# Two-bank cumulative sums, fp32 sums at the start, work moved to GpSimd and a new issue order, in a gated recurrence followed by a GEGLU mixture layer

## The chip, the cores and the metric

The kernel runs on one core of a Trainium2 chip. The core's engines are called PE (TensorE, the matrix products), ACT (ScalarE, the functions), DVE (VectorE), POOL (GpSimd) and SP (SyncE, here only a queue of DMA issues). Each runs its own list of instructions in order and waits on semaphores for the others. The metric is the time of one launch in microseconds (us), the median over several runs. Before the change that is 261.7 us (three runs, 261.25 to 261.72).

## The reference

Inputs q, k, v, a_re, a_im are 4 batches x 8 heads x 768 steps x 48 channels in float32. A complex decay a = a_re + i a_im, its magnitude held at 0.999 or less, drives a state for each batch and head, and the state is read with q:

```python
mag = np.sqrt(a_re * a_re + a_im * a_im)
scale = np.minimum(mag, 0.999) / (mag + 1e-06)
a_re_n, a_im_n = (a_re * scale, a_im * scale)
for t in range(S):
    new_re = ar * S_re - ai * S_im
    new_im = ar * S_im + ai * S_re
    kv = k[:, :, t] outer v[:, :, t]
    S_re, S_im = (new_re + kv, new_im)
    y[:, :, t] = q[:, :, t] @ S_re
```

(ar and ai are column t of a_re_n and a_im_n, the two products are written here without their index strings.) The 3072 x 384 result x goes through a gated feed-forward layer with 1536 hidden channels:

```python
g = x @ w_gate
gelu = 0.5 * g * (1.0 + erf(g * inv_sqrt2))
val = x @ w_val
ffn_out = gelu * val @ w_out
res_gate = 1.0 / (1.0 + np.exp(-(x @ w_res)))
return (x + res_gate * ffn_out)
```

## The kernel before

**Tiling.** The 768 steps are cut into 6 chunks of 128. A tile is one chunk of one batch: 128 steps in the partitions, 8 heads x 48 = 384 channels along the free dimension. There are 24 tiles, worked in units: the first chunk of batches 0 and 1 singly, that of batches 2 and 3 as a pair, then pairs for each later chunk, and the very last pair as two single units again. That makes 14 units, 10 pairs (128 x 768 operands) and 4 singles (128 x 384). For each unit three functions record steps.

**prepare(p)** loads ar, ai, q, k, vf (L373, SP, 192 KB for each tile) and computes log magnitude and angle of the decay and their running sums. ACT takes ln of ar (L394) into la and exp of its negative (L395); t = exp * ai (tai, L397); the square (L399 on ACT, L401 on DVE); ln(1 + s) (L402); la = 0.5 s + la (L403, DVE). la is capped and split into a rounded part lh (L406) and a rest ll (L408), both in the fast float32 matrix type. PE multiplies each with an upper triangle of ones (L359, two products of 128 x 384 for each tile, summed in PSUM), which gives the running sum along the steps. ACT makes E = exp of it (L423) and Ei = exp of its negative (L424), one instruction for each tile. E's last row goes out to the small tile mr by a DMA on POOL's queue (mrd, L428). The angle t = arctan(t) (L433) gets the angle carried over from the previous chunk added to its first row by a DMA on POOL's queue (carry, L439 or L445); it is split into th and tl (L334 copy and L452) and summed in the same way; "round" (L462, ACT) writes the nearest number of full turns as an integer and "fr" (L464, DVE) takes the turns off, one instruction each for each tile. abs (L471 or L473) and two sines (L477) give sine and cosine in CS. DVE multiplies q by E and k by Ei (qe, L482) and both by CS (feat, L487) to the feature tiles fQ and fK, whose heads have 96 channels. These are transposed to QT and KT, for part of the tiles on PE (L504) with a copy on ACT or DVE (L333, L334), for others by a DMA transpose on SP.

**attend(p)** makes the scores of QT and KT for each head (L535), masks them (am, L538), multiplies with v (L547) and with the state (L549), builds the products of features and v (L559) and carries the state on: U (L565), Gb in bfloat16 (L567, DVE) and Gf in float32 (L572). The copies of the result x (L333, L334) end it.

**forward(p)** transposes x (L591 on PE, or by DMA on SP, L583), forms gate and value products (gv, L605) of two of the twelve column tiles of 128 at a time into one PSUM bank each, gelu on ACT (L610) and its product with the value on DVE (h, L611); the residual gate (L620, tanh L622); the output product in three groups of four (L631); ot (L635, DVE), the sum with x (otx, L638, POOL or DVE) and the store (L640). In a pair a bank holds 2 x 256 columns; in a single unit 2 x 128, half a bank.

**The order of the work.** Steps aren't issued as they are recorded. ORDER lists all of them by number and fixes the order on every engine; PLACE sets by step number the engine of those steps that can run on more than one. When a step is issued, its buffers are chosen from what is free (25 wide ones of 128 x 768 float32, tag "wd"; eight PSUM banks, tag "pb"; smaller ones). Where the function set of ACT changes, a table load is issued (L652). The weights wg, wv, wr and wo are loaded by DMAs on POOL's queue (L340), whose issues stand between POOL's other work as ORDER has them. And steps of DVE and POOL whose kind is in PORT are made to take turns by semaphores:

```python
if t.kind in PORT and t.eng in ("DVE", "POOL"):
    other = turn.get("POOL" if t.eng == "DVE" else "DVE")
    if other is not None:
        after(ins, other)
    turn[t.eng] = ins
```

Of the kernel before, what the change touches and what calls it, by code (L numbers as in the profile page):

```python
# [9 lines left out]
FP = mybir.dt.float32  # L10
# [11 lines left out]
SL, ST = 1,1  # L22
WD = 25
# [7 lines left out]
    24: "DVE", 33: "DVE", 40: "DVE", 50: "DVE", 51: "ACT", 53: "ACT", 64: "ACT", 104: "POOL", 114: "ACT", 116: "POOL",  # L31
    132: "ACT", 145: "ACT", 190: "DVE", 191: "DVE", 203: "DVE", 213: "DVE", 223: "DVE", 225: "ACT", 236: "DVE", 252: "ACT",
    305: "DVE", 306: "DVE", 318: "DVE", 322: "ACT", 323: "POOL", 330: "DVE", 340: "DVE", 345: "DVE", 347: "ACT", 353: "DVE",
    422: "DVE", 435: "DVE", 438: "POOL", 446: "DVE", 460: "DVE", 463: "ACT", 551: "DVE", 554: "POOL", 555: "POOL", 562: "DVE",
    572: "DVE", 576: "DVE", 585: "DVE", 595: "DVE", 667: "DVE", 670: "ACT", 671: "POOL", 686: "ACT", 688: "DVE", 692: "DVE",
    771: "DVE", 786: "POOL", 787: "POOL", 821: "DVE", 866: "DVE", 872: "DVE", 899: "DVE", 902: "POOL", 903: "POOL", 910: "DVE",
    933: "DVE", 984: "DVE", 1014: "ACT", 1015: "POOL", 1050: "DVE", 1088: "DVE", 1121: "ACT", 1124: "POOL", 1125: "POOL",
    1151: "DVE", 1160: "DVE", 1198: "DVE", 1232: "POOL", 1233: "POOL", 1240: "DVE", 1251: "ACT", 1257: "DVE", 1304: "DVE",
    1325: "POOL", 1329: "DVE", 1344: "DVE", 1376: "DVE", 1396: "ACT", 1397: "POOL", 1410: "ACT", 1448: "DVE",
}  # L40
ORDER = [
    97, 98, 16, 102, 293, 17, 103, 410, 104, 21, 105, 22, 106, 294, 23, 24, 411, 179, 115, 295, 34, 35, 116, 296, 117, 107, 25,
    178, 118, 303, 26, 36, 420, 27, 37, 108, 119, 28, 100, 181, 180, 413, 304, 109, 120, 421, 110, 305, 121, 38, 29, 188, 30,
    111, 39, 306, 412, 307, 32, 99, 182, 189, 308, 112, 309, 190, 31, 125, 191, 319, 310, 101, 526, 41, 321, 122, 40, 19, 18,
    123, 320, 42, 113, 183, 299, 204, 422, 124, 205, 127, 130, 33, 527, 423, 436, 206, 43, 207, 528, 20, 529, 184, 44, 126, 314,
    192, 46, 128, 316, 193, 210, 45, 322, 208, 424, 194, 47, 195, 49, 211, 323, 131, 129, 199, 52, 196, 209, 48, 536, 315, 311,
    212, 324, 135, 425, 50, 537, 1, 185, 298, 137, 437, 54, 200, 132, 114, 138, 538, 312, 136, 198, 325, 313, 326, 426, 55, 327,
    300, 759, 297, 186, 758, 53, 7, 141, 56, 133, 197, 539, 139, 328, 643, 642, 213, 134, 201, 214, 51, 329, 60, 438, 140, 57,
    216, 439, 58, 144, 202, 2, 187, 330, 215, 334, 12, 552, 217, 8, 332, 553, 6, 0, 219, 331, 218, 226, 336, 142, 220, 768, 333,
    143, 222, 227, 145, 224, 62, 440, 761, 645, 644, 301, 302, 225, 335, 441, 223, 769, 554, 221, 242, 343, 443, 59, 555, 61,  # L50
    339, 243, 63, 240, 652, 64, 344, 444, 341, 233, 231, 442, 241, 228, 234, 317, 244, 445, 653, 146, 760, 337, 5, 342, 232,
    559, 540, 340, 874, 4, 654, 3, 245, 150, 235, 154, 560, 338, 556, 875, 561, 236, 85, 170, 360, 87, 152, 350, 156, 166, 203,
    345, 148, 361, 81, 354, 65, 171, 9, 10, 168, 446, 11, 83, 229, 162, 427, 73, 13, 164, 158, 77, 67, 75, 351, 417, 416, 160,
    557, 89, 355, 541, 79, 90, 69, 358, 74, 431, 558, 230, 71, 151, 318, 359, 770, 251, 364, 348, 365, 66, 155, 153, 349, 433,
    428, 432, 68, 362, 429, 14, 76, 363, 771, 430, 163, 655, 346, 82, 86, 70, 147, 84, 78, 347, 157, 656, 149, 249, 72, 165,
    167, 252, 159, 237, 172, 250, 884, 367, 15, 238, 357, 257, 91, 885, 88, 169, 269, 352, 80, 562, 542, 784, 447, 657, 92, 415,
    253, 239, 161, 448, 261, 543, 414, 273, 173, 366, 93, 353, 563, 564, 668, 877, 369, 174, 658, 450, 876, 434, 669, 254, 94,
    175, 368, 452, 263, 255, 449, 258, 265, 277, 259, 455, 986, 419, 418, 278, 451, 459, 267, 533, 988, 279, 256, 886, 785, 457,
    456, 275, 453, 458, 274, 280, 454, 1206, 370, 670, 435, 659, 372, 464, 374, 386, 460, 271, 671, 246, 465, 530, 382, 887,
    276, 260, 248, 1097, 388, 376, 390, 466, 461, 467, 384, 474, 476, 480, 544, 95, 1207, 392, 247, 531, 356, 475, 786, 547,  # L60
    270, 371, 468, 545, 532, 477, 548, 549, 787, 272, 469, 675, 1096, 772, 373, 262, 266, 281, 481, 987, 773, 546, 1216, 672,
    660, 534, 646, 989, 484, 535, 176, 676, 264, 268, 888, 550, 677, 478, 470, 788, 471, 479, 791, 566, 889, 663, 462, 662, 661,
    792, 96, 673, 282, 793, 287, 1106, 674, 375, 996, 568, 565, 288, 283, 463, 789, 665, 997, 485, 387, 567, 1107, 664, 647,
    473, 284, 177, 289, 391, 571, 575, 573, 377, 389, 285, 790, 900, 396, 394, 649, 648, 577, 290, 551, 678, 1098, 393, 486,
    998, 679, 572, 569, 286, 574, 680, 510, 570, 506, 487, 378, 764, 291, 576, 901, 681, 1208, 592, 650, 488, 774, 490, 511,
    397, 775, 1099, 502, 380, 492, 383, 590, 482, 683, 504, 498, 508, 591, 385, 593, 881, 651, 1306, 1209, 902, 582, 491, 999,
    395, 500, 903, 689, 379, 489, 586, 685, 381, 493, 483, 690, 1000, 594, 398, 583, 1108, 686, 776, 779, 907, 765, 595, 778,
    580, 587, 399, 581, 781, 780, 908, 1217, 596, 794, 601, 400, 904, 578, 682, 584, 472, 777, 880, 292, 1378, 684, 404, 905,
    597, 499, 1109, 579, 585, 909, 600, 1218, 687, 1311, 503, 688, 628, 691, 405, 762, 401, 763, 599, 666, 906, 1122, 696, 890,
    507, 692, 706, 795, 402, 698, 406, 505, 697, 501, 403, 693, 512, 699, 1379, 878, 1012, 589, 520, 610, 509, 1219, 796, 911,  # L70
    708, 494, 407, 1013, 618, 707, 408, 602, 709, 879, 614, 782, 598, 798, 513, 612, 629, 620, 992, 995, 1123, 604, 496, 1307,
    616, 495, 710, 700, 603, 766, 797, 891, 895, 767, 892, 619, 896, 799, 497, 1001, 521, 701, 893, 1383, 910, 716, 615, 800,
    1384, 711, 617, 1385, 1312, 894, 897, 605, 522, 783, 913, 1014, 514, 801, 611, 802, 810, 805, 898, 1313, 515, 806, 882, 717,
    1124, 523, 702, 607, 703, 621, 712, 516, 1015, 912, 1230, 613, 803, 606, 726, 804, 517, 1215, 899, 1002, 914, 993, 883, 994,
    990, 622, 1003, 608, 807, 728, 667, 588, 734, 811, 915, 808, 738, 730, 722, 991, 917, 736, 723, 916, 732, 624, 609, 814,
    623, 824, 713, 918, 740, 724, 815, 812, 822, 1314, 1016, 1004, 1213, 625, 813, 725, 825, 1220, 1006, 1019, 823, 1007, 727,
    694, 731, 524, 518, 1125, 809, 1033, 695, 1020, 1315, 729, 816, 1017, 525, 920, 919, 1021, 636, 817, 1018, 704, 1009, 1008,
    1005, 1316, 735, 1025, 519, 1102, 828, 718, 626, 637, 705, 720, 733, 737, 714, 926, 638, 1231, 1386, 832, 826, 1022, 639,
    719, 818, 630, 1026, 827, 627, 1308, 1210, 833, 1100, 927, 640, 715, 829, 1322, 721, 1129, 631, 1024, 936, 1126, 924, 937,
    641, 921, 632, 1394, 925, 1127, 739, 1232, 1130, 819, 633, 1381, 1023, 928, 1128, 929, 1028, 744, 752, 746, 934, 742, 747,  # L80
    753, 842, 1027, 1221, 1131, 1387, 1110, 741, 409, 831, 935, 1031, 1032, 1323, 1395, 844, 1309, 1030, 846, 754, 1132, 938,
    1222, 944, 939, 1317, 1111, 1112, 848, 743, 1223, 858, 834, 847, 1103, 836, 1113, 945, 745, 859, 1045, 838, 748, 930, 755,
    634, 835, 840, 1029, 1046, 849, 1324, 1114, 1047, 922, 830, 1212, 1048, 1133, 843, 1117, 1233, 1211, 1101, 635, 923, 931,
    1134, 837, 839, 1224, 950, 845, 1325, 1105, 1310, 749, 1038, 850, 1318, 1119, 1116, 1118, 841, 1319, 1115, 1136, 1104, 1320,
    1036, 1039, 946, 851, 966, 756, 1321, 1225, 1037, 1226, 1049, 757, 1135, 1380, 854, 972, 1050, 821, 852, 1214, 948, 853,
# [21 lines left out]
class Store:  # L107


    def __init__(self, tag, bufs):  # L110
        self.tag, self.bufs, self.users, self.tile, self.index = tag, bufs, [], None, None
# [75 lines left out]
def kernel(  # L187
# [13 lines left out]
    nc = tc.nc  # L201
# [78 lines left out]
    class Wide(Val):  # L280
# [7 lines left out]
        def tile(self):  # L288
            if self.store.tile is None:
# [3 lines left out]
                elif self.name in ("E", "Ei", "fr", "fw"):  # L293
                    x = x[:, :].rearrange("p (c m) -> p c m", c=2)
# [388 lines left out]
```

## Time and profile before

| what | value |
| --- | --- |
| median of three runs | 261.7 us (261.25 to 261.72) |
| the profiled execution | 262.78 us, of which the span of the core is 261.0 |
| mean granted PE clock | 0.978 |
| PE busy | 226.4 us, 87% |
| DVE busy | 225.4 us, 86% |
| ACT busy | 214.1 us, 82% |
| POOL busy | 94.5 us, 36% |
| largest DMA queue (SP's) | 35.53 MB, 79.4% of 16 engines |
| gate and value products (L605) | 1008, together 115.1 us busy |
| output products (L631) | 288, 56.5 us busy |
| table loads (L652) | 36, 1.283 us each |

The lines are read so. Busy time counts the instructions themselves, not the waits. PE's products overlap, so the mean length of one is longer than its share of the time (an output product: 326 ns mean, four in 0.65 us on the chain). In the slices of the span each digit is the busy share in tenths, and PEclk the granted clock in tenths. The chain of waits lists from the end backwards what each piece of work waited for.

### The profile page before, as it was taken

What the parts mean: (1) busy time and instruction counts of PE and PEld (TensorE: products, weight loads), DVE (VectorE), ACT (ScalarE), POOL (GpSimd) and SP (SyncE); (2) the same over time, 40 slices, a digit from 0 to 9 for tenths busy, and PEclk for the clock granted to TensorE, in tenths of its full rate; (3) what the DMA queues carried; (4) which work ended last, traced back from release to release, by engine and by line L of the source; (5) the groups of instructions that cost most, each with busy time, mean ns of one, the idle gap of its engine ahead of it and who ended that gap; (6) DMA issues with size and microseconds to landing.
All of it is one profiled execution on the core that took longest, in us unless ns stands there. A gap on an engine that the chain in (4) does not pass through costs nothing.

```text
span 261.0 us, 6358 instructions
## 1 busy us (share of the span) xinstructions
PE 226.4 (87%) x2426; PEld 181.8 (70%) x2426; DVE 225.4 (86%) x404; ACT 214.1 (82%) x355; POOL 94.5 (36%) x114
## 2 busy tenths in 40 slices
PE   0230992889999999999999999999999999999993
PEld 0120772778978977877878877778778777887881
DVE  2589889999899999999999999999999794965363
ACT  4999999899899999999998999999988684241240
POOL 3013086196605743576625634351420001110110
PEclk9999996599999999999999999999999999999998
DMA  8999999989999997995989896999757919402111
GB/s 141 187 187 186 187 194 192 213 163 213 202 184 172 167 186 163 221 146 124 211 149 190 148 179 149 182 168 236 133 114 160 117 23 136 133 3 63 60 63 60
DMA packets 162174, 39.83 MB, mean 153 GB/s; under 512 B 155617, under 2 KB 162145, under 8 KB 162145
## 3 DMA queue, kind: packets, MB, share of 16 engines
q1 hardware_dynamic: 157696, 35.53, 79.4%
q0 software_dynamic: 4448, 3.90, 9.3%
q8 instruction: 19, 0.31, 0.5%
q14 instruction: 11, 0.08, 0.1%
HBM read 31.26 MB, written 4.72 MB: 138 GB/s over the span
## 4 chain that ended last, share of the span: by engine, by line
PE 71%; DMA 11%; ACT 9%; DVE 3%; POOL 2%; SPq 1%; issue 1%; POOLq 0%; DVEq 0%
PE pb L605 32%; PE pb L631 17%; PE pb L359 6%; PE pb L620 4%; PE pb L504 4%; PE pb L535 3%; DMA wo<-in_moe_w_out_dram 3%; DMA wv<-in_moe_w_val_dram 2%; DMA ai<-in_a_im_dram 2%; ACT L652 2%; DMA t<-fr 2%; DMA ar<-in_a_re_dram 2%; POOL t L397 1%; PE pb L549 1%; PE pb L547 1%; ACT CS L477 1%
## 5 line engine op out<-in xcount | busy, mean ns | idle before, releaser
L610 ACT ACTIVATE h<-pb 128x512 bf16<-128x512 f32 (+1 forms) x84 | 41.2, 547 | 23.2 <-PE pb L631 13.0
L605 PE MATMUL pb<-xT,wv 128*128 128x256 bf16 (+1 forms) x504 | 58.1, 257 | 0.4 <-DMA wv<-in_moe_w_val_dram 0.4
L605 PE MATMUL pb<-xT,wg 128*128 128x256 bf16 (+1 forms) x504 | 57.0, 257 | 0.0
L631 PE MATMUL pb<-wo,h 128*128 128x384 bf16 x288 | 56.5, 326 | 0.0
L611 DVE SCALAR_TENSOR_TENSOR h<-h,pb 128x512 bf16<-128x512 bf16 (+1 forms) x84 | 48.5, 602 | 4.2 <-PE pb L605 2.8
L605 PEld LDWEIGHTS <-wg 128*128 128x128 bf16 x504 | 42.9, 98 | 7.1 <-issue 0.8
L652 ACT ACT_TABLE_LOAD x36 | 46.2, 1283 | 1.3 <-PEq L667 0.7
L605 PEld LDWEIGHTS <-wv 128*128 128x128 bf16 x504 | 41.9, 98 | 7.5 <-issue 1.3
L638 POOL TENSOR_TENSOR ot<-ot,x 128x384 f32<-128x384 f32 x16 | 14.6, 913 | 65.0 <-DVE Gb L567 23.4
L631 PEld LDWEIGHTS <-h 128*128 128x128 bf16 x288 | 26.3, 97 | 13.0 <-issue 0.4
L538 DVE TENSOR_TENSOR am<-pb,mask 128x512 bf16<-128x512 f32 x48 | 31.9, 680 | 2.9 <-PE pb L535 2.8
L397 POOL TENSOR_TENSOR t<-t,ai 128x768 f32<-128x768 f32 (+1 forms) x10 | 16.0, 1601 | 18.1 <-DVE fK L487 9.0
L504 PE MATMUL pb<-ident,fK 128*128 128x128 bf16 x112 | 10.0, 246 | 13.5 <-DVE fK L487 13.5
L359 PE MATMUL pb<-th,ut_one 128*128 128x384 f32 x24 | 11.3, 471 | 11.4 <-POOL th L334 11.1
L452 POOL TENSOR_TENSOR tl<-t,th 128x768 fp32r<-128x768 f32 (+1 forms) x10 | 16.5, 1656 | 10.4 <-DVE ll L408 7.8
L635 DVE SCALAR_TENSOR_TENSOR ot<-sg,pb 128x384 f32<-128x384 f32 x24 | 13.1, 547 | 6.8 <-PE pb L631 5.0
L504 PEld LDWEIGHTS <-fK 128*128 128x128 bf16 x112 | 8.4, 112 | 15.0 <-DVE fK L487 14.3
L535 PE MATMUL pb<-QT,KT 96*128 96x128 bf16 x192 | 17.7, 225 | 0.5 <-DMA QT<-fQ 0.4
L535 PEld LDWEIGHTS <-KT 96*128 96x128 bf16 x192 | 13.8, 101 | 3.9 <-issue 2.2
L622 ACT ACTIVATE sg<-pb 128x384 f32<-128x384 f32 x24 | 11.6, 502 | 5.3 <-PE pb L620 2.8
L620 PE MATMUL pb<-wr,xT 128*128 128x384 bf16 x72 | 15.5, 326 | 0.0
L423 ACT ACTIVATE E<-pb 128x384 f32<-128x384 f32 x24 | 11.5, 500 | 3.2 <-PE pb L359 3.0
(91 smaller groups left out, 472.2 us busy)
## 6 DMA issues: line engine op xcount, KB each, us to landing
ar<-in_a_re_dram SPq DMA_DIRECT2D x24, 192.0 KB, 4.6
ai<-in_a_im_dram SPq DMA_DIRECT2D x24, 192.0 KB, 4.6
k<-in_k_dram SPq DMA_DIRECT2D x24, 192.0 KB, 4.4
q<-in_q_dram SPq DMA_DIRECT2D x24, 192.0 KB, 4.5
vf<-in_v_dram SPq DMA_DIRECT2D x24, 192.0 KB, 4.3
out_dram<-ot SPq DMA_DIRECT2D x24, 192.0 KB, 2.8
wg<-in_moe_w_gate_dram POOLq DMA_DIRECT2D x6, 192.0 KB, 5.6
wv<-in_moe_w_val_dram POOLq DMA_DIRECT2D x6, 192.0 KB, 5.9
```

What stands on the lines that cost most here:

```text
L359: nc.tensor.matmul(out=bank.tile, lhsT=ut_one, rhs=x[:, i * DM:(i + 1) * DM], start=(j == 0), stop=(j == 1))
L397: add(e1, "tai", lambda: on[e1].tensor_tensor(out=F("t"), in0=F("t"), in1=flat(T("ai"), n), op=OP.mult), [s["ai"]], [s["t"]], n)
L452: add(e10, "tl", lambda: on[e10].tensor_tensor(out=F("tl"), in0=F("t"), in1=F("th").bitcast(FP), op=OP.subtract), [s["t"], s["th"]], [s["t ...
L504: nc.tensor.transpose(out=tp.tile[:, h, :], in_=s[g].tile[:, i * H + h], identity=ident)
L535: nc.tensor.matmul(out=ap.tile[:, h, :], lhsT=kT.tile[0:DD, u * H // 2 + h, :], rhs=qT.tile[0:DD, u * H // 2 + h, :], start=True, stop=True)
L538: add("DVE", "am", lambda u=u, am=am, ap=ap: nc.vector.tensor_tensor(out=am.tile[:, u * H // 2:(u + 1) * H // 2, :], in0=ap.tile, in1=mask ...
L605: nc.tensor.matmul(out=o_.tile[:, u, :], lhsT=w_[:, k_, (2 * m + u) * 128:(2 * m + u + 1) * 128], rhs=s["xT"].tile[:, k_, 0:n].rearrange(" ...
L610: add("ACT", "gelu", lambda gp=gp, hv=hv: nc.scalar.activation(out=hv(), in_=gp.tile, func=AF.Gelu), [gp], [hh], n, "G")
L611: add("DVE", "h", lambda vp=vp, hv=hv: nc.vector.scalar_tensor_tensor(out=hv(), in0=hv(), scalar=0.5, in1=vp.tile, op0=OP.mult, op1=OP.mul ...
L620: nc.tensor.matmul(out=rp.tile, lhsT=s["xT"].tile[:, k_, i, :], rhs=wr[:, k_, :], start=(k_ == 0), stop=(k_ == KF - 1))
L631: nc.tensor.matmul(out=op_.tile, lhsT=s["h2"].tile[:, k_, i * 128:(i + 1) * 128], rhs=wo[:, k_, :], start=(k_ == 0), stop=(k_ == NF - 1))
L652: plan.run(ORDER, lambda table: nc.scalar.preload_act_table_set(ACT_SETS[table]), after)
```

## The change

1. PSUM is one tile of eight banks, and a buffer can be one bank or an aligned pair of banks. Only the running sums of pair units take two banks (TWO = {"cum"}); E, Ei, round and fr of a pair are then one instruction each, reading both banks.
2. Units 0 to 3 (PF_L, PF_T = 4) don't split la and t. la is capped in place and multiplied in one full float32 product with a float32 triangle, t likewise.
3. The loads of ar go straight into la's buffer and ln works in place, so that no wide buffer is taken for ar.
4. In single units a gate or value step fills a whole bank (four column tiles of 128), so gelu and h work on 128 x 512 instead of 128 x 256.
5. Eighteen steps of eight products of the identity with itself are added to PE (WARM = 18), each into a PSUM bank that nothing reads.
6. The multiplications qe and Gb can be placed on POOL; PLACE puts 13 of 28 qe and 11 Gb there, also 3 squares and 3 more of the last sums; 4 tai, 4 tl and 2 casts of v leave it. ACT gives up copies of KT, QT, x, xT and th, most of them to DVE.
7. ORDER is new throughout, the places of the weight loads in it too.

Groups of four tiles (Quad, "wq") are written but not used, since QUAD is 14, the number of units. The core of the diff, without the lists:

```diff
-SL, ST = 1,1
-WD = 25
+PF_L, PF_T = 4, 4
+WD, WQ = 25, 5
+CSB = 2
+QUAD = 14
+TWO = {"cum"}
+WARM = 18
...
+    psum = psb.tile([128, 8, 512], FP, name="psum")
...
     class Bank(Val):
-        def __init__(self):
+        def __init__(self, width=1):
             Val.__init__(self, plan.store("pb", 8))
+            self.store.width = width
...
+        @property
+        def two(self):
+            return psum[:, self.store.index:self.store.index + 2]
...
-        act("ln", lambda: nc.scalar.activation(out=F("la"), in_=flat(T("ar"), n), func=AF.Ln), [s["ar"]], [s["la"]], "L")
+        act("ln", lambda: nc.scalar.activation(out=A("la"), in_=A("la"), func=AF.Ln), [], allv("la"), "L", N4)
...
-        if SL:
+        if p >= PF_L:
             add("DVE", "lh", ...
...
+        pair = n == 2 and "cum" in TWO
+        cb = Bank(2) if pair else None
+        clm = [cb.part() if pair else Bank() for _ in range(n)]
         for i in range(n):
-            if SL:
-                add("PE", "cumL", lambda i=i: sums(clm[i], i, F("lh"), F("ll")), [s["lh"], s["ll"]], [clm[i]])
+            to = lambda i=i: cb.two[:, i, 0:DM] if pair else clm[i].make([128, DM])
+            if p >= PF_L:
+                add("PE", "cumL", lambda i=i, to=to: sums(to(), i, F("lh"), F("ll")), [s["lh"], s["ll"]], [clm[i]])
             else:
+                add("PE", "cumL4", lambda i=i, to=to: nc.tensor.matmul(out=to(), lhsT=ut_f, rhs=P("la", p)[:, i],
+                                                                       start=True, stop=True), [V["la"][p]], [clm[i]])
-            act("pexpE", lambda i=i: nc.scalar.activation(out=T("E")[:, i], in_=clm[i].tile, func=AF.Exp), [clm[i]], [E[i]], "L", 1)
+            if pair and i == 0:
+                continue
+            r_ = slice(0, 2) if pair else slice(i, i + 1)
+            frm = lambda i=i: cb.two[:, :, 0:DM] if pair else clm[i].tile.rearrange("p (c m) -> p c m", c=1)
+            act("pexpE", lambda r_=r_, frm=frm: nc.scalar.activation(out=T("E")[:, r_], in_=frm(), func=AF.Exp), clm if pair else [clm[i]], E[r_], "L", len(E[r_]))
...
-            add("DVE", "qe", lambda g=g, src=src, mag=mag: nc.vector.tensor_tensor(
+            e12 = place("DVE")
+            add(e12, "qe", lambda g=g, src=src, mag=mag, e12=e12: on[e12].tensor_tensor(
...
-                add("DVE", "Gb" if c else "Gb0", lambda nb=nb, src=src, mb=mb: nc.vector.tensor_tensor(
+                e11 = place("DVE") if c else "DVE"
+                add(e11, "Gb" if c else "Gb0", lambda nb=nb, src=src, mb=mb, e11=e11: on[e11].tensor_tensor(
...
+        w = 512 // (n * 128)
...
     weights()
+    for _ in range(WARM):
+        wb = Bank()
+
+        def f(wb=wb):
+            wb.make([128, 512])
+            for _ in range(8):
+                nc.tensor.matmul(out=wb.tile[:, 0:128], lhsT=ident, rhs=ident, start=True, stop=True)
+        add("PE", "warm", f, (), [wb])
```

## The prediction

> **What bounds the kernel now.** I read the page first (busy shares, then the 40 slices), then the busy time of each engine by stretch, then the chain that ended last, and at the end single groups for prices. The page:
>
> ```profile
> PE 226.4 (87%) x2426; PEld 181.8 (70%) x2426; DVE 225.4 (86%) x404; ACT 214.1 (82%) x355; POOL 94.5 (36%) x114
> PEclk9999996599999999999999999999999999999998
> DMA  8999999989999997995989896999757919402111
> ```
>
> Three engines look alike over the whole span, so the share decides nothing; and the clock is low only in slices 7 and 8, with the DMA engines near full up to some 80 us. By stretch (columns: length, then busy us and number of instructions on PE, PEld, DVE, ACT, POOL, then clock, DMA, GB/s):
>
> ```profile
> 30.00:40.00 10.00, 9.11 (x60) 7.17 (x58) 8.78 (x15) 9.85 (x21) 5.56 (x5) 1.00 1.31 186
> 40.00:50.00 10.00, 4.69 (x58) 4.24 (x58) 9.90 (x16) 9.21 (x12) 5.23 (x8) 0.56 1.24 208
> 50.00:60.00 10.00, 9.09 (x121) 7.35 (x120) 10.00 (x20) 9.50 (x17) 8.25 (x9) 0.93 0.98 177
> 60.00:70.00 10.00, 9.57 (x162) 8.56 (x160) 8.98 (x19) 8.74 (x22) 5.65 (x7) 1.00 1.21 209
> 80.00:120.00 40.00, 40.00 (x453) 33.28 (x451) 39.27 (x66) 39.48 (x68) 21.68 (x20) 1.00 1.04 179
> 120.00:160.00 40.00, 40.00 (x440) 32.61 (x438) 39.80 (x69) 39.00 (x63) 23.27 (x27) 1.00 0.89 164
> ```
>
> From 80 us on PE never stops; before 50 us it is ACT and DVE that never stop, fed by the DMAs. The chain (start, length, what) names the hand-over:
>
> ```profile
> 49.77 5.38 DMA ai<-in_a_im_dram
> 55.64 1.10 POOL wv L340 x2
> 56.73 1.76 POOL t L397
> 58.50 5.66 DMA wv<-in_moe_w_val_dram
> 64.21 0.51 PE pb L605 x6
> ...
> 70.11 7.25 DMA wo<-in_moe_w_out_dram
> 77.40 1.46 PE pb L631 x8
> 78.86 1.97 PE pb L605 x18
> ...
> 93.10 0.65 PE pb L631 x4
> 93.75 0.69 PE pb L359 x4
> ...
> 253.44 3.26 PE pb L631 x20
> 256.70 0.02 issue
> 256.72 0.57 DVE ot L635
> ```
>
> So the end is set by when PE gets its weights and what it still owes then. PE's real pace is in these rows: 0.65 us for 4 out products of 128x384 (0.163 each), 1.97 for 18 gv products of 256 columns (0.109), 0.69 for 4 sums (0.172). With 0.056 for each 128-column product ("0.67 PE pb L605 x12"), summing the products in issue order gives what is still owed at first use: 201.0 us at the first wg product (55.4 us by the tile's first start), 193.4 at the first wv (64.21), 186.7 at the first wo (70.9), 180.3 at the third wo (77.40). Added to the times: 256.4, 257.6, 257.6, 257.7; PE really ends at 256.7. PE has no air from 55 us on. A change counts by how it moves those four starts and what is owed at them; whatever it frees on ACT or DVE later is idle time only.
>
> **The change, part by part.** The profiled execution took 262.78 us: span 261.0 and 1.78 around it; it is 1.08 above the 261.7 median. I work in its span and put the difference on 261.7.
>
> *Merged pair instructions.* For 10 pairs, E, Ei and round go from two of 128x384 to one of 128x768 (60 ACT instructions to 30), fr from 20 to 10. By busy means (0.50 against 0.84) that saves 0.16 each, 4.8 us; but the chain has two E in 0.76 and one 768 exponential in 0.73, so the pace gains 0.03, in all 0.9 us of ACT. The Trainium skill ("ScalarE: Activation LUTs", What ACT_TABLE_LOAD costs) says that back-to-back activations overlap by about 93 ns; by that the 30 merges are an estimated 2.8 us, and the row goes below it. On DVE 10 x (2 x 0.543 - 0.95) = 1.4 by means. A two-bank read waits for both sums, one more at 0.17 to 0.34 us; PE's queue has other work there. Half of all this comes after 80 us and is worth nothing.
>
> *Wider gelu and h in the four single units.* 24 of each of 256 columns become 12 of 512: ACT 24 x 0.396 - 12 x 0.607 = 2.2 us, DVE 24 x 0.414 - 12 x 0.68 = 1.8. Two of the units come first (55 to 70 us), two last, where 20 out products (3.26 us) follow the last gelu, so that its extra 0.2 us is covered. Uncovered it would cost just that.
>
> *No split for units 0 to 3.* lh, ll, th and tl go (ll 0.95, lh 0.55 for a pair), a cap (about lh's 0.55) stays, and 24 split products at 0.172 become 12 in full fp32. None is in the trace. Low end 0.172 each, one pass; high end 0.69, twice the pair of passes replaced; the small fp32 products of L521 run at 242 ns for 16 columns and cannot decide. I take 0.66 (the dear end, as the first sums stand on the chain: "14.56 1.02 PE pb L359 x2"): +4 us of PE, all before 50 us where PE is idle over half the time. Latency about even: 0.95 less on DVE, 2 x 0.3 more on PE.
>
> *Eighteen groups of eight idle products on ident.* 144 x 0.056 = 8.0 us of PE; fifteen groups lie before the first wg product, where PE idles, three (1.34 us) after it, where it is owed. Each takes a PSUM bank and so waits for one.
>
> *Work moved.* POOL gains 13 qe (9 x 1.82 + 4 x 1.0, priced as tl), 11 Gb (0.82 as Gf), 3 otx (0.913), 3 sq (1.86 as L397), loses 4 tai, 4 tl, 2 casts: +21.5, to 116 us. DVE loses by its own rows 13 qe (10.8), 11 Gb (6.0), 3 otx, 3 sq (2.9), most of lh and ll; gains tai and five PSUM copies (0.68 each): about -16. ACT gives up 5 transposed copies at 1.01, x, xT and th copies: with the merges -17 by means, -10 by pace. After 80 us PE covers these gains. If that cover went, DVE at 39.8 of 40 us would come next. Every POOL operation named in PORT waits for DVE's last such one and the reverse. The Trainium skill ("SBUF — State Buffer", two separate sides) says that DVE and GpSimd take their shared port pair in turn, one fully blocked. The waits written into this program do the same, so no row shows the lock alone; by that rule the 21.5 us on POOL are taken from DVE's time, which is the mechanism of the slower rival below.
>
> *Loads, carries, stores.* As many as before: 186 on SP, 12 carries on POOL. ln now works in the buffer that ar is loaded to. SP issues in order, so a transpose that waits for its features holds the loads behind it; before 80 us SP stands on the chain for 1 us only ("1.25 0.56 SPq L373" and 0.47 at 49.26), so I put nothing on the new order, and up to one load's 4.6 us if a transpose is early; that lies inside the slower rival.
>
> **The sum.** What PE owes in the new order: 204.8 us at the first wg (three idle groups 1.34, and 2.5 us of transposes and scores that used to come sooner), 192.6 at wv, 184.5 at the first wo, 179.5 at the third.
> First wg: ACT's work ahead of the first gelu is 51.0 us by pace against 52.2 (one table load more, copies fewer), so 55.4 - 1.2 = 54.2, and 259.0.
> wv: the third wv issue stands behind a carry that needs arctan 48.7 us into ACT's work; with ACT's 6.9 us of idle (59.1 less 52.2) that is 55.6, plus carry 0.8, mr 0.66, issue 0.6: 57.7, landing 5.66 later, 63.3; 255.9.
> First wo: after the last wv issue (59.5) POOL has th 0.82, two tl 3.64, one qe 1.82 and the issue 0.8: 66.6, where before it followed wv at 61.63 at once. Landing 7.25 later is 73.9, and 258.4. Third wo: mr and two issues more, 68.8, 76.1, 255.6.
> The latest are wg 259.0 and wo 258.4, where the latest before was 257.7. I put 0.3 on the later one for POOL's waits: 259.3, so 1.6 later. **Forecast 261.7 + 1.6 = 263.3 us**, with its own range 262.3 to 266.
>
> **Rivals.**
> *Faster: PE starts earlier.* The idle products keep the clock up, and ACT's waits for ar (2.9 us of its idle before 59 us) go, if the new order of loads brings ar sooner. PE's 4.69 busy us in the 40 to 50 stretch at 0.56 would be 2.6 at full clock, 2.1 less ahead of the first x. Both together put wg's road at 259.0 - 5.0 = 254.0; wo's road, which hangs on POOL, gains the 2.9 alone, 258.4 - 2.9 = 255.5, so 2.2 better than 257.7: 259.5. Were all roads to gain 5.0, it would be 258.0. For it: the low clock is in the rows, and ACT has 9.2 to 9.9 of 10 us busy there. Against: ACT's waits for PE are 1.7 us in all up to 59 us, so a faster PE has little to give. The Trainium skill ("TensorE: Matmul & The Clock Gate", Part 1) states half speed until PE has been busy for some microseconds; the 0.56 agrees, and by that factor the 4.69 us would be 2.3, an estimate that gains 2.3 in place of 2.1.
> *Much slower: POOL's queue.* Four SBUF operations (6.3 us) now stand between wv and wo on POOL. Eight tl of a pair idle 10.4 us on POOL in the trace, nearly all for DVE, 1.3 each. Waiting so at each of four, the first wo is issued 5.2 later and PE ends at 263.6: 261.7 + 6.2 = 267.9. It decides from 0.6 us of waiting on. Against it: DVE's own work is 16 us lighter over the span.
> *No change.* The hand-over is set by landings of DMAs that run near 187 GB/s either way, and the roads meet within 0.5 us of the old: 261.7.
>
> **How the numbers follow.** Forecast 0.36, POOL's queue 0.22, earlier start 0.35, nothing 0.07. So faster by over 0.2% (0.5 us, about what three runs of 261.25 to 261.72 can tell) 0.35, same 0.07, slower 0.58. The range goes from the far end of the earlier start, 258.0, to POOL's queue, 267.9, and a little over, 268.3.
>
> **What would show it.** Right: the first wg product near 54 us, the first out product of a wo near 74, PE full from there, its end near 259; ACT and DVE busy times 10 to 17 us lower with more idle after 80 us; POOL at about 116. The first wo used before 71 and a clock of 1.0 in 40 to 50 speak for the faster case; idle on POOL before its qe or tl between 58 and 70 us for the slow one. I would be wrong altogether if PE had holes after 80 us: then DVE or POOL port waits feed it too late and the four starts no longer count.

## The result

The changed kernel takes 264.72 us (median of four runs, 264.52 to 265.14) against 261.52 us for the kernel before (four runs, 261.25 to 261.72): ratio 1.0125, 95% interval 1.0107 to 1.0143. It is 3.2 us slower. The forecast was 263.3, slower, with a range of 258.0 to 268.3. Ratios are taken over fast runs alone, while the medians listed under the experiments are over all runs, of which x6 and x7 have one slow one each (264.73 and 268.53 without it).

The profiled execution of the changed kernel took 264.91 us, with a span of 263.1. That is 2.1 more than the span before, not 3.2, because the profiled execution of the kernel before (262.78 us) was 1.26 us over its median and this one is only 0.2 over. The forecast span was 261.0 + 1.6 = 262.6.

The page of the changed kernel: busy times, clock and DMA share in the 40 slices.

```profile
PE 236.8 (90%) x2570; PEld 188.8 (72%) x2570; DVE 213.5 (81%) x359; ACT 203.4 (77%) x303; POOL 112.7 (43%) x135
PEclk9999559999999999999999999999999999999999
DMA  8999999999999998899959896598959609410211
```

DVE and ACT have 12 and 11 us less work than before, POOL has 18 more, PE 10 more, and the time does not follow ACT's and DVE's savings. By stretch (the columns as before: PE, PEld, DVE, ACT, POOL, clock, DMA, GB/s):

```profile
0.00:10.00 10.00, 1.89 (x16) 1.62 (x16) 3.12 (x9) 4.58 (x7) 1.24 (x11) 1.00 1.05 156
20.00:30.00 10.00, 4.45 (x19) 2.68 (x18) 7.33 (x15) 9.92 (x15) 4.56 (x5) 0.75 1.44 186
30.00:40.00 10.00, 8.33 (x51) 5.62 (x51) 8.96 (x16) 9.58 (x13) 3.75 (x7) 0.56 1.30 200
40.00:50.00 10.00, 8.92 (x128) 7.47 (x126) 10.00 (x17) 9.94 (x16) 7.99 (x11) 1.00 1.08 187
50.00:60.00 10.00, 8.78 (x144) 8.09 (x143) 10.00 (x17) 9.97 (x16) 9.51 (x12) 1.00 1.07 187
60.00:70.00 10.00, 8.35 (x135) 7.16 (x133) 9.23 (x16) 9.79 (x15) 8.35 (x8) 1.00 1.08 193
160.00:200.00 40.00, 40.00 (x431) 32.20 (x430) 38.03 (x65) 31.23 (x48) 15.92 (x21) 1.00 0.80 152
```

ACT starts later (4.58 busy us of the first ten, 6.36 before), then is full from 10 to 60 us, and the low clock has moved from 40-50 to 20-40. After 160 us the time saved on ACT is idle time (31.2 of 40 where it was 37.4). The chain of waits at the hand-over (start, length, what):

```profile
54.18 0.82 POOL v L382
55.00 0.35 POOL wv L388
...
57.40 1.51 POOL wv L388 x3
58.91 8.35 DMA wv<-in_moe_w_val_dram
67.30 0.79 PE psum L727 x11
...
255.83 3.27 PE psum L757 x20
```

The load of wv that PE waits for (1.2 us, until 67.30) is issued last of the six and takes 8.35 us to land; before, the one on the chain took 5.66. The first use of each weight, and the start of the last output product, by the tiles' first and last starts:

| kernel | first wg | first wv | first wo | last output product |
| --- | --- | --- | --- | --- |
| before | 55.4 | 64.2 | 70.9 | 256.4 |
| changed | 52.6 | 65.9 | 75.0 | 258.8 |

So PE gets its first weights 2.8 us sooner, its second 1.7 later and its third 4.1 later.

### The profile page after: what moved, and what is told of

The parts are those of the page before. It is cut to its first block, busy times and chain, and to the rows that moved or that the text cites. A ratio compares the mean times of both kernels' runs of the same rounds, so it can differ in the third digit from the quotient of the medians.

```text
span 263.1 us, 6594 instructions
## 1 busy us (share of the span) xinstructions
PE 236.8 (90%) x2570; PEld 188.8 (72%) x2570; DVE 213.5 (81%) x359; ACT 203.4 (77%) x303; POOL 112.7 (43%) x135
## 4 chain that ended last, share of the span: by engine, by line
PE 67%; ACT 10%; DMA 8%; DVE 8%; issue 3%; POOL 2%; SPq 1%; ACTq 0%; DVEq 0%; POOLq 0%
PE psum L727 32%; PE psum L757 16%; PE psum L406 4%; PE psum L746 4%; PE psum L646 3%; DMA wv<-in_moe_w_val_dram 3%; DMA t<-fr 3%; ACT L787 2%; PE psum L614 2%; DMA la<-in_a_re_dram 2%; ACT t L473 2%; ACT CS L483 2%; PE psum L663 2%; PE psum L665 2%; ACT s L470 1%
## 5 line engine op out<-in xcount | busy, mean ns | idle before, releaser
L735 ACT ACTIVATE h<-psum 128x512 bf16<-128x512 f32 x72 | 39.9, 606 | 27.1 <-PE psum L727 26.6
L736 DVE SCALAR_TENSOR_TENSOR h<-h,psum 128x512 bf16<-128x512 bf16 x72 | 47.2, 680 | 15.9 <-PE psum L727 8.1
L727 PE MATMUL psum<-xT,wv 128*128 128x256 bf16 (+1 forms) x504 | 56.9, 257 | 1.7 <-DMA wv<-in_moe_w_val_dram 1.2
L727 PE MATMUL psum<-xT,wg 128*128 128x256 bf16 (+1 forms) x504 | 56.1, 257 | 0.0
L757 PE MATMUL psum<-wo,h 128*128 128x384 bf16 x288 | 56.0, 326 | 0.0
L727 PEld LDWEIGHTS <-wv 128*128 128x128 bf16 x504 | 42.3, 98 | 8.5 <-issue 1.6
L727 PEld LDWEIGHTS <-wg 128*128 128x128 bf16 x504 | 42.6, 98 | 6.8 <-issue 0.6
L650 DVE TENSOR_TENSOR am<-psum,mask 128x512 bf16<-128x512 f32 x48 | 31.7, 682 | 6.2 <-PE psum L646 6.2
L592 POOL TENSOR_TENSOR Ke<-k,Ei 128x768 bf16<-128x768 f32 (+1 forms) x9 | 13.9, 1546 | 18.0 <-DVE fQ L597 6.5
L646 PE MATMUL psum<-QT,KT 96*128 96x128 bf16 x192 | 18.1, 223 | 1.6 <-DVE KT L382 1.0
L746 PE MATMUL psum<-wr,xT 128*128 128x384 bf16 x72 | 15.3, 326 | 0.0
L775 PE MATMUL psum<-ident 128*128 128x128 bf16 x144 | 12.4, 242 | 2.2 <-POOL ident masks.py:199 1.5
```

What stands on the lines that cost most here:

```text
L592: add(e12, "qe", lambda g=g, src=src, mag=mag, e12=e12: on[e12].tensor_tensor(out=T(g + "e")[:, 0:n * H].rearrange("p x u d -> p (x u d)") ...
L646: nc.tensor.matmul(out=o_[:, h, :], lhsT=kT.tile[0:DD, u * hh + h, :], rhs=qT.tile[0:DD, u * hh + h, :], start=True, stop=True)
L650: add("DVE", "am", lambda u=u, am=am, ap=aps[u]: nc.vector.tensor_tensor(out=am.tile[:, u * hh:(u + 1) * hh, :], in0=ap.tile, in1=mask.to_ ...
L727: nc.tensor.matmul(out=x[:, u, :], lhsT=w_[:, k_, (w * m + u) * 128:(w * m + u + 1) * 128], rhs=s["xT"].tile[:, k_, 0:n].rearrange("p c t ...
L735: add("ACT", "gelu", lambda gp=gp, hv=hv, fro=fro: nc.scalar.activation(out=hv(), in_=fro(gp), func=AF.Gelu), parts["wg"], [hh], k2 + 1, "G")
L736: add("DVE", "h", lambda vp=vp, hv=hv, fro=fro: nc.vector.scalar_tensor_tensor(out=hv(), in0=hv(), scalar=0.5, in1=fro(vp), op0=OP.mult, o ...
```

## The experiments

Each kernel ran beside the kernel before on the same chip. Ratios are to that kernel before (medians 261.38 us for x1 to x4, 262.58 for x5 to x8, 262.3 for x9 to x11 and y1), so they are compared with the 1.0125 of the change, and a difference in us is worked out from the ratios unless it says otherwise. "First wg" and so on are read as in the table above.

| run | median us | ratio and interval | first wg, wv, wo | last output product |
| --- | --- | --- | --- | --- |
| x1_wv_order | 264.32 | 1.0098 [1.0069, 1.0127] | 52.5, 66.2, 74.2 | 258.0 |
| x2_late_idle | 265.14 | 1.0146 [1.0104, 1.0189] | 52.6, 66.0, 74.4 | 258.8 |
| x3_no_idle | 264.65 | 1.0106 [1.0068, 1.0144] | 52.9, 66.2, 74.6 | 258.5 |
| x4_wv_late | 263.96 | 1.0109 [1.0063, 1.0155] | 52.6, 65.8, 73.8 | 257.5 |
| x5_qe_gb_dve | 292.54 | 1.1163 [1.1128, 1.1198] | 56.3, 72.4, 81.7 | 287.8 |
| x6_two_instr | 265.26 | 1.0107 [1.0076, 1.0137] | 52.7, 67.3, 75.7 | 259.7 |
| x7_wv_early | 268.64 | 1.0225 [1.0179, 1.0271] | 52.5, 68.7, 76.9 | 262.6 |
| x8_split_la | 271.13 | 1.0336 [1.0308, 1.0364] | 60.0, 73.3, 81.4 | 265.0 |
| x9_wv_six | 266.05 | 1.0140 [1.0115, 1.0165] | 52.5, 65.5, 74.0 | 259.9 |
| x10_first_load | 266.8 | 1.0167 [1.0134, 1.0199] | 52.6, 65.8, 74.6 | 259.3 |
| x11_wd24 | 266.81 | 1.0167 [1.0149, 1.0185] | 54.5, 68.3, 76.1 | 260.1 |
| y1_before_idle | 266.11 | 1.0134 [1.0112, 1.0157] | 55.5, 65.3, 71.9 | 260.0 |

### The order of the wv loads, and the idle products (x1 to x4)

The theory was the one of the prediction: PE's end is its first wg product, plus the work it then owes, plus its holes. The rival was that another engine stands close behind PE, so that what PE saves turns into waits. The wv loads are steps 3 to 5 (first half of the columns) and 9 to 11 (second half). The changed list issues 3, 10, 5, 11, 9, 4, and the first wv product needs 3, 4 and 5. The idle products are steps 16 to 33; in the trace twelve of the groups run before the first wg product, three up to the first wv and three at 117 us.

x1: the two loads change places.

```diff
+_a, _b = ORDER.index(10), ORDER.index(4)
+ORDER[_a], ORDER[_b] = 4, 10
```

> The six wv loads are issued 3, 10, 5, 11, 9, 4 in the changed kernel, and the first wv product needs 3, 4 and 5; here 4 and 10 change places. Theory (PE's debt: end = first wg product + work owed + holes): the wait of 1.2 us for wv goes, first wv products run through from about 65.9, the end is 1.2 to 1.4 us earlier, ratio to the kernel before about 1.007 in place of 1.0125. Rival (gelu and h feed PE, so a hole closed early opens again later): under 0.4 us.

x2: three groups cut (x3 has a plain 1 for all eighteen; x4 is x1 and x2 together).

```diff
-            for _ in range(8):
+            for _ in range(1 if 16 + z in (16, 27, 31) else 8):
```

> The three groups of idle products that PE runs near 117 us are cut from eight products to one each, 21 products of 0.056 us. Theory (PE's debt): 1.2 us earlier, ratio about 1.008. Rival (PE is fed there by others and the idle products fill holes): within 0.3 us of the changed kernel.

> All eighteen groups of idle products are cut to one product each. Theory (PE's debt): as the run with the three late groups cut, 1.2 us earlier than the changed kernel, since the three groups between first wg and first wv end in the wait for wv, which only gets longer, and the twelve earlier ones lie in idle time. Rival (the idle products keep the clock up): the granted clock of the first 50 us falls below that of the changed kernel (1.00, 1.00, 0.75, 0.56, 1.00 by 10 us) and the end is 1 to 2 us later than with only the late groups cut.

> Both: wv loads 4 and 10 exchanged and the three late idle groups cut. Theory (PE's debt): the two add up, 2.4 to 2.6 us earlier than the changed kernel, ratio about 1.003. Rival (one hole takes the place of another): no more than the better of the two alone.

None of the four is told from the changed kernel by its ratio: all four intervals overlap 1.0107 to 1.0143. For x2 and x4 the theory's ratios (1.008 and 1.003) lie outside the intervals; for x1 and x3 (1.007 and 1.008) they lie just inside, so those two runs alone do not refute it. In the single traces x1 lost the wait for wv, and the last output product starts 0.8 us sooner, but a new wait for wo of 1.0 us stands in the list of PE's waits. x2 has 1.2 us less to do and ends at the same 258.8. Its waits of PE from 66 us on (who waited for what: us, times, longest):

```profile
PE psum L646 <- DMA QT<-fQ: 0.8, 1, 0.8
PE psum L727 <- DMA wv<-in_moe_w_val_dram: 0.5, 1, 0.5
PE psum L727 <- DVE h L736: 0.3, 1, 0.3
PE psum L406 <- DVE x L382: 0.2, 1, 0.2
```

The wait for QT and the one for x (the first and last line) aren't there in the changed kernel. The three groups also come 0.9 us sooner (115.2 us for 116.1), so 2.1 us are lost behind them, and the list names 1.0 of it. Here the rival holds: the time taken off PE turns into waits. That PE is short of time by less than a microsecond is a reading of this one trace. The two edits together (x4) start the last output product 1.3 us sooner, half of the 2.4 to 2.6 expected, and that is one trace.

x3 bears on the clock. Without idle products the clock in the first fifty microseconds is 1.00, 1.00, 0.70, 0.61, 0.83, with them 1.00, 1.00, 0.75, 0.56, 1.00, and the end is not told apart. The stretch from 30 to 40 us in x3, then in x2:

```profile
30.00:40.00 10.00, 6.94 (x37) 4.21 (x36) 8.93 (x15) 9.55 (x13) 3.65 (x7) 0.61 1.35 203
30.00:40.00 10.00, 6.96 (x58) 4.81 (x57) 8.90 (x14) 9.51 (x13) 3.60 (x7) 0.83 1.30 198
```

Up to the first wg product x2 has the same idle products as the changed kernel, and yet shows 0.82 and 0.83 between 20 and 40 us where that shows 0.75 and 0.56; x9, with the same ones again, shows 0.70 and 0.61. So one trace differs from the next by more than x3 differs from the changed kernel, and no effect of the idle products on the clock before 40 us is shown. Nor did a higher clock help: the first wg product is at 52.6 in x2 as in the changed kernel. From 40 to 50 us the clock is 1.00 in both of these and 0.83 in x3, whose first wg product comes 0.3 us later; no gain at the end is shown for that.

### The idle products in the kernel before (y1)

One part of the change alone: eighteen such steps in the kernel before, at like places.

```diff
+for _n, _i in reversed(list(enumerate((28, 50, 90, 97, 104, 116, 130, 142, 166, 204, 229, 251, 278, 289, 314, 650, 650, 650)))):
+    ORDER.insert(_i, 1450 + _n)
```

> The kernel before with eighteen groups of eight idle products added to PE: twelve ahead of the first wg product, three between it and wv, three near 117 us. Theory (PE's debt, 0.3 us of holes from 55.4 on): 1.3 to 2.7 us later than the kernel before, ratio 1.005 to 1.010, the clock between 40 and 50 us above 0.56. Rival (as in the run without the late groups, other waits take up what the idle products leave): within 0.7 us; rival (the clock decides): 1 to 2 us earlier.

This costs 3.8 us, 1.0134, as much as the whole change and more than the 1.3 to 2.7 expected. The start does not move (first wg at 55.5). From there the groups cost what they weigh: the first wv product is 1.1 us later, the first wo product 1.0, the last output product 3.6. The six groups behind the first wg product are 48 x 0.056 = 2.7 us; the rest fits a longer wait, 1.9 us where it was 0.4. PE's waits from 66 us on, in this kernel and then in the kernel before:

```profile
PE pb L538 <- DMA KT<-fK: 1.9, 1, 1.9
```

```profile
PE pb L535 <- DMA QT<-fQ: 0.4, 1, 0.4
```

The clock between 40 and 50 us rose from 0.56 to 0.66, with no gain. So adding work to PE costs its full price in the kernel before, and a wait besides; taking the same work out of the changed kernel (x2, x3) returns nothing that can be measured. Both fit one reading, that other engines stand close behind PE, but no run shows which engine. One rival is left: every group also takes one of the eight PSUM banks, in y1 as in x2 and x3, where one product of each group stays, and no run takes the banks away.

### wv earlier still (x7, x9)

x7 adds to x1 that half of wv is issued ahead of POOL's two qe, and cuts all six groups behind the first wg product.

```diff
+for _k in (3, 4, 5):
+    ORDER.remove(_k)
+_i = ORDER.index(12) + 1
+ORDER[_i:_i] = [3, 4, 5]
```

> wv loads 4 and 10 exchanged, loads 3, 5 and 4 issued directly behind wr, ahead of POOL's two qe, and the six groups of idle products behind the first wg product cut to one product each. Theory (PE's debt): with no wait for wv left, PE comes to the first wv product 1.2 us sooner than 65.9 and the end is 1 us earlier than with the exchange and the three late groups, 2 us earlier than the changed kernel. Rival (ACT and DVE, full from 40 to 70 us, set PE's pace there): the removed products turn to idle time, the end is that of the exchange alone, 0.7 us earlier than the changed kernel.

It is 1.0225, some 2.6 us worse than the change instead of 2 better. Landing of the vf loads issued from 42 to 45 us, in the changed kernel and then in x7:

```profile
DMA to landing us min/median/max: 7.7/9.3/10.7
```

```profile
DMA to landing us min/median/max: 8.6/12.3/14.0
```

Then POOL's timeline of x7 (start, length; in brackets the idle time ahead of it) and DVE's:

```profile
57.36 0.82 POOL L389 CAST v<-vf 128x768 bf16<-128x768 f32 x1 [3.74 <-PE psum L753]
```

```profile
58.21 0.96 DVE L604 TENSOR_TENSOR fQ<-Qe,CS 128x1536 bf16<-128x1536 bf16 x1 [3.27 <-POOL v L389]
```

Three loads of 192 KB moved ahead of vf are 3 x 1.05 us at the 187 GB/s of these stretches, and vf lands 3.0 to 3.3 us later. POOL's cast of v comes at 57.36, not 54.18; the trace names PE's product, but the cast also reads vf, whose landing fits. DVE's next PORT step has to take its turn behind that cast and stands 3.3 us; PE then stands 3.6. x9 leaves the wv loads where the exchange of x1 has them and keeps the six cuts.

> The changed kernel with wv loads 4 and 10 exchanged and all six groups of idle products behind the first wg product cut to one product each; wv is issued where it stood. Theory (loads queue up: the earlier wv of the last attempt put 3.2 us of transfers in front of vf, and this alone cost it its time): the run is as good as the one with the exchange and the three late groups, or up to 1 us better, 262.9 to 263.9 us. Rival (the cut of the three middle groups is what cost it): 266 us or more.

At 266.05 us it meets the rival's 266 in absolute time; the kernel before is 0.9 us slower on this chip than on that of x1 to x4, though. By the ratio, 1.0140, it is not told from the changed kernel, nor from x4 (1.0109), and it is below x7, if only just (1.0165 against 1.0179 at the nearest ends of the intervals). The gain that the theory expected is not there. Its vf isn't late (the cast of v is at 53.90). So the early issue costs, and cutting the three middle groups gains nothing. PE has 42 products less than the changed kernel, 2.4 us, and its busy time fell by 0.7 (236.77 to 236.05); where the rest went, the lists of waits don't name. The first wo product is 1.0 us sooner than in the changed kernel and the last output product 1.1 later, so the time is lost in between. Which engine sets PE's pace then I have not shown; DVE, at 10.00 of 10 us from 40 to 60 and at 9.4 to 10 of 10 from 70 to 160 in these traces, is the candidate.

### POOL's new work back to DVE (x5)

```diff
-            e12 = place("DVE")
+            e12 = "DVE"
-                e11 = place("DVE") if c else "DVE"
+                e11 = "DVE"
```

> All qe and Gb go back to DVE, nothing else changes: 30 us leave POOL, 17 us come to DVE. Theory (PE's debt at the weights): before 60 us DVE has no room (10.0 of 10 us busy from 40 to 60), and three of the qe lie there, 0.95 each, so the first wg product comes 1 to 2 us later than 52.6; wv and wo are issued 2 to 4 us earlier; after 80 us nothing shows. End 0 to 1.5 us later than the changed kernel. Rival (POOL's longer queue and the turns between POOL and DVE are the loss): 1.5 to 3 us earlier than the changed kernel, about the kernel before.

Both were far off: 292.54 us. DVE's busy time goes up by 15 us (213.5 to 228.4), the time by 27. Two stretches of x5:

```profile
40.00:60.00 20.00, 15.20 (x198) 13.29 (x196) 17.55 (x29) 17.58 (x24) 11.54 (x17) 0.83 1.08 187
80.00:120.00 40.00, 35.20 (x357) 28.65 (x354) 34.58 (x57) 33.09 (x49) 11.16 (x13) 0.91 0.84 147
```

No engine is full in either. PE waits for DVE (h 9.6 us in all with L727 and L614, am 7.8), DVE for ACT, PE and POOL in turn. The list was made for 24 operations on POOL; with them on DVE, what stands behind them in line comes late. So x5 shows what this list costs without its placement, and not what the placement would be worth in a list made for DVE. It also answers the question of the wv issue: POOL, with nothing to do, waited 4.0 us for vf and cast v at 54.19, as in the changed kernel at 54.18. The two qe ahead of wv on POOL's queue had cost wv nothing.

```profile
54.19 0.83 POOL L382 CAST v<-vf 128x768 bf16<-128x768 f32 x1 [3.96 <-DMA vf<-in_v_dram]
```

### One exponential for both tiles (x6)

```diff
-act("pexpE", lambda r_=r_, frm=frm: nc.scalar.activation(out=T("E")[:, r_], in_=frm(), func=AF.Exp), ...
+act("pexpE", lambda r_=r_, frm=frm: [nc.scalar.activation(out=T("E")[:, k:k + 1],
+    in_=frm()[:, k - r_.start:k - r_.start + 1], func=AF.Exp) for k in range(r_.start, r_.stop)][-1], ...
```

(Ei, round and fr likewise.)

> E, Ei, round and fr of the pairs are issued as two instructions of 128x384 again, in the same places and the same two banks. Theory (pace: two in 0.76, one in 0.73): ACT's busy time up by 3 to 5 us, its pace by 1 us in all and 0.3 before the first gelu; end 0 to 0.5 us later than the changed kernel. Rival (means: 0.16 each, and ACT is full up to 60 us, with nine of them there): first gelu and end 1.4 us later.

The ratio, 1.0107, is that of the change. ACT's busy time goes from 203.4 to 204.6 us for 30 more instructions, 0.04 each and well under the 3 to 5 us expected, and DVE's from 213.5 to 214.3 for ten; the first wg product is at 52.7, the first gelu at 57.7 (57.4 in the changed kernel). So the pace, not the mean durations, was the right price, and the merging bought nothing measurable. The single trace has its first wv product 1.4 us later, because POOL waited for vf (1.61 us ahead of its cast of v); whether that comes from the split is not shown.

### The split of la, and the wide buffers (x8, x11)

x8 splits la of units 0 to 3 again.

```diff
-            add("DVE", "cap", lambda: nc.vector.tensor_scalar(out=PF("la", p), in0=PF("la", p), ...
+            add("DVE", "cap", split, [V["la"][p]], [s["lh"], s["ll"]], n)
...
-to=to: nc.tensor.matmul(out=to(), lhsT=ut_f, rhs=P("la", p)[:, i],
+to=to: sums(to(), i, F("lh"), F("ll")), [s["lh"], s["ll"]], [clm[i]])
```

> Units 0 to 3 split la into lh and ll again and sum it in two fast products; t stays in full fp32. Theory: PE has room there, so the fp32 products (0.61 each) cost nothing and the split costs DVE 2.7 us in the first 35 us, where it is 67 to 90% busy: end 0 to 0.7 us later than the changed kernel. Rival (fp32 products delay the early chain): 0.5 to 1 us earlier.

It costs 5.5 us on top of the change's (6.4 by the medians), where 0 to 0.7 was expected. DVE has 3.0 us more to do, but the first wg product is 7.4 us later. The waits of SP's queue from 5 to 60 us, changed kernel and then x8:

```profile
SPq L436 <- PE psum L646: 3.7, 1, 3.7
SPq L436 <- DVE la L503: 1.4, 1, 1.4
```

```profile
SPq L436 <- POOL t L463: 4.8, 1, 4.8
SPq L436 <- PE psum L406: 3.4, 2, 2.6
SPq L436 <- DVE v L382: 1.9, 1, 1.9
```

The loads wait 11.2 us in all, 7.0 in the changed kernel, 3.4 of it for the sums that read lh and ll. That these hold buffers which the loads want is a reading of this list; the longest wait, 4.8 us, is for POOL. x11 tests the buffers alone, with one wide buffer less (24 for 25).

> The changed kernel with 24 wide buffers in place of 25. Theory (wide buffers gate the loads; the split of la cost 6 us because lh and ll hold buffers, and the SP queue waited 4 us more): loads wait, the first wg product comes 0.5 to 3 us later, and so does the end. Rival (buffers are ample, the split cost DVE time and order): within 0.3 us of the changed kernel.

1.0167 [1.0149, 1.0185] against 1.0125 [1.0107, 1.0143], 0.4% or 1.1 us later, with the first wg product at 54.5, 1.9 later. The buffers do gate the loads. They don't account for all of x8 by this measure; what share the 3 us on DVE and the order have in it stays open.

### The first load (x10)

```diff
+ORDER.remove(168)
+ORDER.insert(ORDER.index(167) + 1, 168)
```

> As the run with the exchange and six groups cut, and the first load of all, ai, is issued behind the two ar loads that ACT's first ln waits for. Theory (ACT is full from 10 to 60 us, so the first load sets everything): ACT starts at about 5.5 in place of 6.08, the first wg product and the end come 0.5 us earlier than in that run. Rival (DVE, which needs ai, then starts later by the same): no change.

266.8 us and 1.0167 against 1.0140 in x9: no gain, the intervals overlap, and the first wg product stays (52.6 and 52.5). ACT's first ln did start sooner, at 5.10 for 5.97, but ACT then waited 1.16 us for the next ar, and from 7.5 us on it stands where it stood. No change, as the rival said, though the trace shows the wait for ar and not DVE as what took the gain.

## Why the prediction was right, and where it was not

- **That PE bounds from the first wg product on**: borne out where work is added (y1), not where it is taken away (x2, x3). From 80 to 120 us PE has 0.54 us of holes, a wait for h; holes after 80 us were named as the sign of being wrong altogether, and these are small.
- **The sum of roads to 259.3**: PE's last product ends at 259.1, but that the two lie so close is in part luck. With the measured starts and the work that the prediction puts at them, the roads are 52.6 + 204.8 = 257.4 for wg, 65.9 + 192.6 = 258.5 for wv and 75.0 + 184.5 = 259.5 for wo. The latest road is wo's and not wg's, on which the forecast stood: wg came 1.6 us sooner than forecast, wo 1.1 later, and the errors cancelled. Against the kernel before PE starts 2.8 us sooner, owes 3.8 more and ends 2.4 later, so 1.4 us of holes came in; the wait for wv is 1.2.
- **1.6 us later**: 3.2 by the medians, 2.1 in the spans. The sum was for the profiled execution of the kernel before; 1.1 of the missing 1.6 us is that this one was 1.26 over its median and the changed one only 0.2, and 0.5 is in the spans.
- **First wg at 54.2**: 52.6. I tied it to ACT's work ahead of the first gelu. That gelu came at 57.45 (51.0 + 6.45 of idle; I had used 6.9), but the wg products don't wait for it. In the trace PE waits 1.03 us for KT, a copy on DVE, runs scores of QT and KT and eight idle products, and then the first wg product without a wait; xT had been ready since 49.
- **wv at 63.3**: 65.9, then a wait to 67.30. I let the third load release the first product, while the list issues the one it needs last, and took the old landing of 5.66 where it was 8.35. Two wrong terms; x1 shows that even so the wait decided little, as the next one stood behind it.
- **First wo at 73.9, third at 76.1**: 75.0 for the first. POOL waited 1.63 us for a carry between wv and wo, of which 0.3 was reckoned. A wait on POOL between wv and wo was the slower rival's mechanism, but that one was for DVE and priced at 5.2 us; this is for a DMA, at a third of it.
- **Idle products**: fifteen before the first wg and three behind was wrong: twelve, three, and three at 117 us. The work owed had counted them rightly; "three idle groups 1.34" was half of it. Had I seen that 2.7 us of the 3.8 more that PE owed were idle products, 2.7 of the 3.8 us of y1 could have been forecast.
- **Merging, 0.03 each**: right; x6 gives 0.04 of ACT's busy time. The Trainium skill ("ScalarE: Activation LUTs", What ACT_TABLE_LOAD costs) says that back-to-back activations overlap by about 93 ns, an estimated 2.8 us for the thirty; the run has 1.2.
- **Busy times**: ACT 10.7 us less, as by pace (10); DVE 11.9 less (16 forecast), POOL 18.2 more (21.5 forecast).
- **fp32 product 0.66**: about right at PE's fast pace, and in PE's idle time as said. The trace lists each product as two instructions, 12 at L515 for the six tiles of units 0 to 3. Four instructions, so two products, start at 18.93 us and the next work at 20.28, 0.68 for a product; at 12.47 us the same number takes twice as long (the next work starts at 15.19). The 0.61 in what was expected of x8 is one instruction's.

```profile
18.93 1.51 PE L515 MATMUL psum<-la,ut_f 128*128 128x384 f32 x4
```

- **No split, "latency about even"**: it was priced as DVE and PE time alone. In this list x8 puts it at 5.5 us, and x11 puts one wide buffer at 1.1 of them. The term was mis-sized.
- **"After 80 us PE covers these gains. If that cover went, DVE would come next"**: x5 shows 27 us, with PE waiting for DVE more than for any other engine after 80 us. In this list the place of that work is worth far more than its busy time.
- **The faster rival** failed as argued: the clock of 40 to 50 us did come to 1.00, and ACT's wait for ar did not go, it grew from 2.9 to 4.5. x3 shows no effect of the idle products on the end that can be measured.

What stays open is why the changed kernel is still about 1.1% slower than before with its idle products cut to one of eight (x3). There PE starts at 52.9 and owes 204.8 less 42 x 0.056 us, so it would end at 255.3 without holes; it ends at 258.8. Of these 3.5 us the lists of waits name 1.8 (xT 0.4, wv 0.5, x 0.4, QT 0.3, h 0.2). The traces also show PE's later wv and wo (1.7 and 4.1 us in the changed kernel); no run brought those back to the old times. No version here beats the kernel before.

## What to carry to other kernels

When one engine runs full from some point on, time its start, count what it still owes, and look up which transfer releases that start, by its place in the queue and not by its kind. Here work added to that engine cost its price and a wait besides (y1), and work taken away gave nothing back that could be measured (x2, x3), so the two directions have to be tried apart. In a list written for one placement, a step can't be priced by its busy time: also count the buffers that it holds, the loads that it is put in front of (x7: three loads of 192 KB, 3.0 to 3.3 us), and the engine that has to take its turn behind it.

## What the hardware showed that I had not expected

Eight idle products at a time from 1.5 us on did not hold the clock: it was 0.75 and 0.56 between 20 and 40 us with them in one trace and 0.82 and 0.83 in another (x2), 0.70 and 0.61 without, with PE busy 4.45 and 8.33 us of ten in the first. In x11, where PE was busy for 6.64 us between 30 and 40 us, it was 0.50. The 1.00 of the first ten microseconds is not borne out by the products: sixteen idle ones from 1.46 us on take 1.89 us, 0.12 each, while eight from 52.19 us on are followed by the next work at 52.64, 0.056 each. And 15 us more of DVE work with no engine full made 27 us more of time, while PE's clock was 0.91 from 80 to 120 us, where PE was busy for 35.2 of 40.
